# Eight of 32 softmax heads by another road: scores once, exp with queries on partitions, 32x32 transposes on VectorE, product with v in sixteen 32x32 tiles

## The chip, the cores and the metric

The kernel runs on one core of a Trainium2 chip. The time is the device time of one execution in microseconds, from the first to the last instruction; three runs were taken of the kernel before. The engines are TensorE (PE in the profile, its weight loads PEld), VectorE (DVE), ScalarE (ACT), GpSimd (POOL) and SyncE (SP), which issues all DMAs of this kernel in the order in which they are written.

## The reference

```python
# x: 2048 x 1024, 32 heads of 32; all in fp32
def _A_ref(x, wqkv, wo):                    # linear attention
    pq, pk = phi(q), phi(k)                 # phi(t) = where(t > 0, t + 1, exp(t)) + 1e-6
    kv = jnp.einsum("bhsd,bhse->bhde", pk, v)
    z = jnp.einsum("bhsd->bhd", pk)
    o = (pq @ kv) / (pq @ z + 1e-6)
    return o @ wo
def _B_ref(x, wqkv, wo):                    # softmax attention
    scores = jnp.einsum("bhqd,bhkd->bhqk", q, k) * (Dh ** -0.5)
    o = jnp.einsum("bhqk,bhkd->bhqd", _softmax(scores, axis=-1), v)
    return o @ wo
g = sigmoid((x * gate_w).sum(-1, keepdims=True))
return g * _A_ref(x, A_wqkv, A_wo) + (1 - g) * _B_ref(x, B_wqkv, B_wo)
```

## The kernel before

**Linear work.** Each fp32 product with a weight matrix is three matmuls of 128x128 by 128x512 on operands split into a high and a low part (`three`, L151 to L153). A "unit" is one tile of 128 rows times 512 columns: 8 steps over the inner dimension, 24 matmuls. Eighty units lie in the first part (v of heads 0 to 15: 16 units, then q and k of branch B: 64), and 144 come later through the generator `linear`: v of the other heads (16), keys and values of branch A ("kv", 64), queries of A ("q", 32), output of A ("o", 32). The last 32, B's output, come through `output`.
From "kv" on a unit needs the split x of its rows from DRAM (`load_xp`, L473), in one of two buffers. The q stage also rebuilds A's output weights (`mix`, L559, whose parts are stored by L569) and turns its result by four transposes per unit (`queries`, L597). Each kv unit is followed by eight products of 32 x 32 (L498).

**A softmax head, before.** Scores are computed twice. `maxima` has queries on the partitions: 64 matmuls of 128x512 (L791), each with a maximum over its row on VectorE (L796). The negated maxima are turned (L807), and go as two extra rows into the q operand, so that the second pass gives scores less their maximum. `heads_` has keys on the partitions: 64 matmuls (L942), each with an exp on ScalarE (L946) into one of seven tiles `pr`. Three times a head, `av` multiplies five or six of these tiles with v: four matmuls of 32 columns of v by 512 queries side by side in column strips, per block of 128 keys (L1038; each fp32 matmul is two records in the profile). The sum over keys is made by elementwise adds of the `pr` tiles: their first 1536 columns on GpSimd (L987, L991; 1792 columns for heads that begin while `linear` is at "q"), the rest on VectorE (L998, L1000), then a matmul with ones (L844), reciprocals (L851) and a product (L854).

**What sets the order.** Nothing is scheduled by the machine: every engine runs the list that the program wrote. A planner in the kernel writes it, from costs per instruction (`MM`, `AV` and so on) and a clock for each engine (`T`). It advances four generators, "lin", "max", "head", "out", and each time takes the one furthest behind its due time (`behind`, `AHEAD`); VectorE work that may wait is put off and filled in (`defer`, `fill`). Eight PSUM banks: six in a ring for single products, two (4 and 7) held for `av` and VectorE's sums. The head loop starts when the v units of heads 16 to 31 and one head's maxima plus 12 are done, and "lin" is then spread over all 32 heads by rates per score (2.6 matmuls in the q stage).

Of the kernel before, what the change touches and what calls it, by code (L numbers as in the profile page):

```python
# [9 lines left out]
F32 = mybir.dt.float32  # L10
# [21 lines left out]
AHEAD = {"head": 0, "max": 6, "lin": 9, "out": 0}  # L32
# [9 lines left out]
NMID = 14  # L42


@with_exitstack
def kernel(
# [50 lines left out]
    v_d = [dram.tile([P, NT, C], F32, name=f"v{c}") for c in range(NQC)]  # L97
    wa_d = [[[dram.tile([HK, P, C], F32, name=f"wa{p}_{a}_{c}") for c in range(NQC)] for a in range(NK // HK)]
# [18 lines left out]
    dn = [sb.tile([P, C // DH], F32, name=f"dn{i}") for i in range(2)]  # L117

# [96 lines left out]
    RING = [0, 1, 2, 3, 5, 6]  # L215
# [98 lines left out]
    def v_out(c, t, ps):  # L314
        va = mid[10 + t % 2]
        nc.scalar.copy(va, ps)  # L316
        nc.sync.dma_start(v_d[c][:, t, :], va)

# [78 lines left out]
    for n, (g, j, sec) in enumerate(order):  # L397
# [7 lines left out]
        split(hi, lo, ps, nc.vector)  # L405
# [26 lines left out]
    lin_kind = [chunks[0][0]]  # L432

# [29 lines left out]
    def load_xp(n):  # L463
        if n in xp_done:
            return
        xp_done.add(n)
        i, t = units[n]
        kind = chunks[i][0]
        xp_ready[n % 2] = 0.0
        if kind != "v":  # L470
            xp_ready[n % 2] = T["pe"] + 4.0
            for p, src in enumerate(oA_d if kind == "o" else xs):
                nc.sync.dma_start(f32(blocks(xp_t[n % 2], p)), src[t])  # L473
# [102 lines left out]
    def keysum(c):  # L576

        yield lambda: both(bank_at(), z_end[c % 2])
# [32 lines left out]
    def linear():  # L611
# [4 lines left out]
        for n, (i, t) in enumerate(units):  # L616
            kind, c = chunks[i]
            follow = chunks[i + 1] if i + 1 < len(chunks) else None
            xp = xp_t[n % 2]
            yield bank_at  # L620
# [8 lines left out]
            if n == (TPC if kind == "v" else 0):  # L629
                load_head(0)  # L630
                load_v(0)
            if n == (TPC + 1 if kind == "v" else 0):
                load_head(1)
                load_v(1)
            for k in range(NK):
                yield lambda: ended(w_left[k], w_ready[k], xp_ready[n % 2])
                need(w_left[k])
                stat = xstat(t, k) if kind == "v" else [blocks(xp, p)[:, k] for p in range(2)]
# [4 lines left out]
                if k == 0 and kind == "v" and c == NQC - 1 and NT - 4 < t < NT - 1:  # L643
                    load_xp(n + 3)
                if k == 0 and n + 7 == len(units) and not o_main[0]:
                    load_o(0)
# [14 lines left out]
                if follow and t == NT - 1:  # L661
                    split_w(*follow, k, *coming_w.popleft(), nc.vector if kind == "v" else nc.gpsimd)
# [6 lines left out]
            if kind == "v":  # L669
                give(b, use("act", 0.5, T["pe"] + LATENCY["pe"]))  # L670
                v_out(c, t, ps)
            elif kind == "kv":
# [18 lines left out]
                if t == NT - 1:  # L691
                    extra = keysum(c)
            elif kind == "q":
# [584 lines left out]
```

## Time and profile before

| | us |
|---|---|
| median of three runs (2920.92 to 2924.22) | 2921.34 |
| span of the profiled execution | 2921.0 |
| mean granted TensorE clock | 0.995 |
| the 80 units of the first part end at about | 442 |
| second-pass scores (L942) | 547 to 2724 |
| after them, what is left of B's output and its storing | 2724 to 2921 |

A row of the timeline or of a group names line, engine, operation, output<-inputs, shape and count; "mean ns" is the length of one record, and since matmuls are pipelined, the distance from one start to the next is what one costs.

### The profile page before, as it was taken

The page shows a single profiled execution, that of the slowest core. Times are in us where ns is not written, and L with a number is a line of the kernel's source. Part 1 is how long each engine was busy: PE and PEld are TensorE (multiplying, and loading weights), DVE is VectorE, ACT ScalarE, POOL GpSimd, SP SyncE. Part 2 cuts the span into 40 slices and gives each one's busy share as a digit, 9 for nine tenths or more (in the row PEclk, how much of TensorE's full clock was granted, in tenths as well). Part 3 has the DMA queues.
Part 4 walks back from the last instruction along what each step waited for, and adds up shares of the span by engine and source line. Part 5 has one row for each costly group of instructions (what it writes and reads, how often), then busy time and mean ns, then how long its engine had stood idle before and what let it go on. Part 6 is the DMA issues. An engine that isn't in the chain of part 4 may idle for free.

```text
span 2921.0 us, 44021 instructions
## 1 busy us (share of the span) xinstructions
PE 2885.7 (99%) x15936; PEld 2073.3 (71%) x15936; DVE 2055.2 (70%) x3451; ACT 1522.7 (52%) x2840; POOL 1772.2 (61%) x582
## 2 busy tenths in 40 slices
PE   9999999999999999999999999789999999999999
PEld 8888888766666666666666767566676666666787
DVE  3222114788888888888888888678888888887522
ACT  4111111466666667666666666556666666666410
POOL 0000001388898889988898888568778878785000
PEclk9999999999999999999999999999999999999999
DMA  6687333322242234233423234545455443523542
GB/s 195 213 268 233 122 116 101 115 87 90 89 132 89 90 91 120 75 89 96 125 90 91 90 117 145 162 157 160 151 157 183 130 145 121 158 87 130 181 154 80
DMA packets 282142, 381.67 MB, mean 131 GB/s; under 512 B 91786, under 2 KB 168074, under 8 KB 278794
## 3 DMA queue, kind: packets, MB, share of 16 engines
q1 hardware_dynamic: 281924, 378.85, 41.9%
q8 instruction: 126, 2.06, 0.3%
q14 instruction: 92, 0.75, 0.1%
HBM read 268.70 MB, written 108.79 MB: 129 GB/s over the span
## 4 chain that ended last, share of the span: by engine, by line
PE 95%; DMA 2%; DVE 1%; ACT 0%; SPq 0%; issue 0%; ACTq 0%
PE bank L942 16%; PE bank L791 16%; PE bank L151 16%; PE bank L153 15%; PE bank L152 15%; PE bank L1038 15%; PE bank L844 1%; DMA big<-xs 0%; PE bank L597 0%; DMA wa<-mid 0%; PE bank L498 0%; DMA big<-oA 0%; DVE big L1004 0%; DMA mid<-in_a_wqkv 0%; DMA big<-in_a_wo 0%; DVE mx L796 0%
## 5 line engine op out<-in xcount | busy, mean ns | idle before, releaser
L991 POOL TENSOR_TENSOR big<-big,big 128x1536 f32<-128x1536 f32 (+1 forms) x434 | 1557.4, 3588 | 209.5 <-ACT big L946 187.4
L796 DVE TENSOR_REDUCE mx<-bank 128x1 f32<-128x512 f32 x2048 | 1312.1, 682 | 334.0 <-PE bank L791 329.9
L946 ACT ACTIVATE big<-bank 128x512 f32<-128x512 f32 x2048 | 1182.1, 602 | 526.7 <-PE bank L942 459.2
L151 PE MATMUL bank<-big,big 128*128 128x512 f32 x2048 | 802.5, 392 | 25.1 <-DMA big<-xs 21.2
L942 PE MATMUL bank<-big,big 128*128 128x512 f32 x2048 | 810.7, 397 | 1.8 <-ACT big L946 1.7
L791 PE MATMUL bank<-big,big 128*128 128x512 f32 x2048 | 803.7, 393 | 2.8 <-ACT mid L316 2.6
L153 PE MATMUL bank<-big,big 128*128 128x512 f32 x2048 | 800.5, 391 | 0.4 <-DVE big L258 0.4
L152 PE MATMUL bank<-big,big 128*128 128x512 f32 x2048 | 800.5, 391 | 0.0
L942 PEld LDWEIGHTS bank<-big,big 128*128 128x128 f32 x2048 | 384.8, 188 | 159.0 <-issue 62.0
L151 PEld LDWEIGHTS bank<-big,big 128*128 128x128 f32 x2048 | 385.4, 188 | 115.2 <-issue 18.9
L1038 PE MATMUL bank<-big,mid 128*32 128x512 f32 x4096 | 459.2, 593 | 0.0
L791 PEld LDWEIGHTS bank<-big,big 128*128 128x128 f32 x2048 | 385.6, 188 | 86.6 <-ACT big L946 3.7
L153 PEld LDWEIGHTS bank<-big,big 128*128 128x128 f32 x2048 | 385.2, 188 | 82.8 <-DVE big L258 1.3
L152 PEld LDWEIGHTS bank<-big,big 128*128 128x128 f32 x2048 | 385.4, 188 | 80.1
L746 POOL MEMSET big<- 32x2048 f32 x3 | 5.4, 1809 | 530.8 <-PE bank L152 459.6
L1038 PEld LDWEIGHTS bank<-big,mid 128*32 128x32 f32 x4096 | 127.7, 110 | 263.7 <-issue 263.7
L1000 DVE TENSOR_TENSOR bank<-bank,big 128x512 f32<-128x512 f32 (+1 forms) x434 | 280.9, 647 | 7.8 <-ACT big L946 6.2
L258 DVE TENSOR_TENSOR mid<-bank,mid 128x512 fp32r<-128x512 f32 x64 | 44.3, 692 | 263.2 <-ACT mid L257 263.2
L987 POOL TENSOR_TENSOR big<-big,big 128x1536 f32<-128x1536 f32 (+1 forms) x31 | 111.7, 3602 | 136.2 <-ACT big L946 136.2
L257 ACT CAST mid<-bank 128x512 fp32r<-128x512 f32 x64 | 37.7, 590 | 291.4 <-PE bank L153 286.5
L851 DVE RECIPROCAL bank<-bank 128x128 f32<-128x128 f32 x128 | 123.4, 964 | 3.5 <-PE bank L844 0.4
L258 DVE TENSOR_TENSOR big<-mid,big 128x512 fp32r<-128x512 f32 x96 | 64.0, 687 | 75.9 <-ACT big L257 75.8
(72 smaller groups left out, 977.9 us busy)
## 6 DMA issues: line engine op xcount, KB each, us to landing
big<-xs SPq DMA_DIRECT2D x192, 512.0 KB
qk<-mid SPq DMA_DIRECT2D x128, 256.0 KB
big<-oA SPq DMA_DIRECT2D x64, 512.0 KB
big<-qk SPq DMA_DIRECT2D x96, 256.0 KB
big<-qk SPq DMA_DIRECT2D x384, 64.0 KB
xs<-big SPq DMA_DIRECT2D x64, 256.0 KB
oA<-mid SPq DMA_DIRECT2D x64, 256.0 KB
mid<-in_b_wqkv SPq DMA_DIRECT2D x48, 256.0 KB
```

Of the source, the lines that this page charges most:

```text
L151: yield nc.tensor.matmul(ps, sh, mh_, start=(kt == 0), stop=False)
L152: yield nc.tensor.matmul(ps, sh, ml_, start=False, stop=False)
L153: yield nc.tensor.matmul(ps, sl, mh_, start=False, stop=(kt == NK - 1))
L791: nc.tensor.matmul(bank[b], q[:, t * P:(t + 1) * P], k[:, j * C:(j + 1) * C], start=True, stop=True)
L796: nc.vector.tensor_reduce(m[:, t, j:j + 1], bank[b], AX.X, ALU.max)
L851: nc.vector.reciprocal(pl[:, sl], pl[:, sl])
L942: nc.tensor.matmul(bank[b], k[:, t * P:(t + 1) * P], q[:, j * C:(j + 1) * C], start=True, stop=True)
L946: nc.scalar.activation(pr_t[i][:, j * C:(j + 1) * C], bank[b], AF.Exp, scale=SCALE)
L987: nc.gpsimd.tensor_add(lacc[:, :qp], pr(0)[:, :qp], pr(1)[:, :qp])
L991: nc.gpsimd.tensor_add(lacc[:, :qp], lacc[:, :qp], pr(t)[:, :qp])
L1000: nc.vector.tensor_add(lacc[:, qp:] if t == NT - 1 else l_b[:, :n], l_b[:, :n], src)
L1038: nc.tensor.matmul(av_b[j * DH:(j + 1) * DH, :], v[:, t, :], pr(t)[:, j * C:(j + 1) * C], start=(t == 0), stop=(t == NT - 1))
```

## The change

Heads 0 to 7 (`NB = 8`) leave the old road; heads 8 to 31 keep it.

- **Scores once** (`bheads`). For each quarter of the queries (512) and each of its four blocks of 128 there are four matmuls of 128 queries by 512 keys, with the same operands as in `maxima`. VectorE takes the negated maximum of each row of 512 keys, ScalarE computes exp(score - maximum) with that maximum as a bias per partition and sums the row (`accum_out`), and VectorE transposes the result in blocks of 32x32 into a tile laid out by key blocks. The maximum is that of the 512 keys alone. The scale is moved into q (`nc.scalar.mul`).
- **Product with v** (`burst`). Once a quarter is complete (16 scores), 256 matmuls of 32x32 by 32x128 follow in one piece, on all 16 tiles of the array: row strip a takes key or query block a, column strip c the keys' quarter c, four PSUM banks. ScalarE copies the four results.
- **Weights and sum** (`weigh`). After a head's four quarters its parts are weighted with exp(maximum of 512 - overall maximum) / sum: small operations on [128, 64], four transposes, four matmuls of 128x512 that spread the factors, four products on GpSimd, and four matmuls that add the parts.
- **Dropped for these heads:** the second score pass with its exp, the turned maxima, `av`, the adds on GpSimd and VectorE, the matmul with ones, the reciprocals.
- **Order.** A new generator "score" is advanced while less than `FEED = 2.4` us of VectorE work is waiting. All eight banks are in the ring until it ends. "lin" fills the rest of that stage with v and kv units only; q waits. v of heads 16 to 31 now reads x back from DRAM as kv does. Then `maxima` and the old head loop run for 24 heads, with q, o and what is left of kv at one rate.
- **Data.** v of the first 16 heads is stored a second time by rows of 32 (four DMAs per tile of 128 rows).

```diff
-AHEAD = {"head": 0, "max": 6, "lin": 9, "out": 0}
+AHEAD = {"head": 0, "max": 6, "lin": 9, "out": 0, "score": 0}
+NB = 8
+EXPB, TRB, AVB, OEV = 0.68, 0.6, 4.3, 0.3
+FEED = 2.4
-    RING = [0, 1, 2, 3, 5, 6]
+    RING = list(range(8))
...
+        if c == 0:
+            for i in range(TPC):
+                nc.sync.dma_start(vh_d[:, :, t * TPC + i, :].rearrange("h i d -> i h d"),
+                                  va[i * DH:(i + 1) * DH, :].rearrange("p (h d) -> p h d", d=DH))
...
+    def burst():
+        n = bursts.popleft()
+        h, J = divmod(n, NJ)
+        bs = [take() for _ in range(4)]
+        end = use("pe", AVB, *(free[b] for b in bs))
+        v = ft[14].rearrange("p (b d) -> p b d", d=DH)
+        for m in range(C // DH):
+            for c in range(NJ):
+                for a in range(4):
+                    rows = slice(a * DH, (a + 1) * DH)
+                    nc.tensor.matmul(bank[bs[a]][c * DH:(c + 1) * DH, :P], v[rows, c * (C // DH) + m, :],
+                                     place(n, c)[rows, m], start=(m == 0), stop=(m == C // DH - 1))
...
+    def bheads():
...
+            for i in range(TPC):
+                for j in range(NJ):
...
+                    nc.tensor.matmul(bank[b], bq[:, J * C + i * P:J * C + (i + 1) * P], k[:, j * C:(j + 1) * C],
+                                     start=True, stop=True)
...
+                    nc.vector.tensor_reduce(m[:, col], bank[b], AX.X, ALU.max, negate=True)
...
+                    nc.scalar.activation(src, bank[b], AF.Exp, bias=m[:, col], accum_out=lb[h % 2][:, col])
...
+                        nc.vector.transpose(place(n, j)[:, :, i, :], src.rearrange("p (m q) -> p m q", q=DH))
...
-    streams = {"lin": linear(), "max": maxima(), "head": heads_(), "out": output()}
+    streams = {"lin": linear(), "score": bheads(), "max": maxima(), "head": heads_(), "out": output()}
...
-    steps = H * NT * NJ
+    steps = (H - NB) * NT * NJ
...
+        if name == "score":
+            work = sum(it.cost for it in later if it.at < T["pe"] + 1.0)
+            return 50.0 if max(T["dve"] - T["pe"], 0.0) + work < FEED else -100.0
         if not begun[0]:
             if name == "lin":
-                return 0.0 if lin_done[0] < warm + 8 * pace else -100.0
+                return 0.0 if lin_next[0] in ("v", "kv") else -100.0
...
+            rate[0] = (warm + sum(cost.values()) - lin_done[0] - RESERVE) / steps
```

TensorE's list, before, in the kv stage: second-pass scores (L942), maxima (L791), linear work (L151 to L153), the eight small products of a kv unit (L498) and a run of `av` (L1038).

```order
L942 MATMUL bank_243<-big_210,big_211 128x512
L151 MATMUL bank_249<-big_226,big_213 128x512
L791 MATMUL bank_245<-big_209,big_222 128x512
L498 MATMUL bank_248<-mid_232,mid_236 32x32 x8
L1038 MATMUL bank_247<-big_3494,mid_241 32x512 x4
L1038 MATMUL bank_247<-big_3495,mid_241 32x512 x4
...
L942 MATMUL bank_244<-big_210,big_211 128x512
L791 MATMUL bank_243<-big_209,big_222 128x512
```

The same stage now, for one of heads 0 to 7: scores (L979), linear work (L161 to L163), kv products (L515), and the first and last rows of a burst (L865).

```order
L515 MATMUL bank_254<-mid_242,mid_244 32x32 x8
L161 MATMUL bank_258<-big_232,big_221 128x512
L979 MATMUL bank_253<-big_219,big_216 128x512
L162 MATMUL bank_258<-big_232,big_221 128x512
L163 MATMUL bank_258<-big_232,big_221 128x512
...
L163 MATMUL bank_258<-big_234,big_221 128x512
L865 MATMUL bank_255<-big_2915,big_2925 32x128
L865 MATMUL bank_254<-big_2915,big_2925 32x128
...
L865 MATMUL bank_253<-big_2918,big_2925 32x128
L515 MATMUL bank_251<-mid_240,mid_244 32x32 x8
L979 MATMUL bank_257<-big_219,big_216 128x512
```

A quarter now has 16 scores among about 60 linear matmuls and then 256 burst matmuls without a break, where before every pair of scores shared its place with one linear matmul. In the whole stage there are 512 scores, 32 bursts and 1908 linear matmuls up to the start of the old head loop; 1500 linear ones are left for its 24 heads and 816 for the last part, as many as before.

VectorE's list, before, in a head: maxima (L796) and adds (L1000).

```order
L1000 TENSOR_TENSOR bank_250<-bank_250,big_3493 128x512
L796 TENSOR_REDUCE mx_200<-bank_249 128x1
L796 TENSOR_REDUCE mx_200<-bank_244 128x1
L796 TENSOR_REDUCE mx_200<-bank_246 128x1
L1000 TENSOR_TENSOR bank_250<-bank_250,big_3494 128x512
```

Now, in heads 0 to 7: maxima (L985), transposes (L995), and the kv stage's operations (L694).

```order
L985 TENSOR_REDUCE mx_202<-bank_258 128x1
L995 STREAM_TRANSPOSE big_2921<-big_2923 128x16x32
L995 STREAM_TRANSPOSE big_2922<-big_2923 128x16x32
L995 STREAM_TRANSPOSE big_2915<-big_2923 128x16x32
...
L694 SCALAR_TENSOR_TENSOR mid_241<-mid_241,bank_253 128x256
L985 TENSOR_REDUCE mx_202<-bank_252 128x1
```

One maximum in four carried an add beside it; now each maximum carries a transpose of the same 512 elements.

SP's list where the first part ends, now: the last stores of q and k, the loads of x for the first two units, and then 24 loads of q and k for head 0, a row of x2 being two of them.

```order
L424 DMA qk_0_7_151<-mid_244 128x512
L425 DMA qk_1_7_159<-mid_246 128x512
L490 DMA big_220<-xs_0_63 128x1024
L490 DMA big_220<-xs_0_79 128x1024
L490 DMA big_221<-xs_1_64 128x1024
L490 DMA big_221<-xs_1_80 128x1024
L776 DMA big_217<-qk_0_0_144 32x512
L776 DMA big_217<-qk_1_0_152 32x512
L776 DMA big_217<-qk_0_0_144 32x512 x2
```

Before, the same place went on with v units out of SBUF, and the loads for head 0 came while these ran.

GpSimd's list in the old head loop, before, kv stage (L987 opens a head).

```order
L991 TENSOR_TENSOR big_3498<-big_3498,big_3497 128x1536
L686 TENSOR_TENSOR mid_235<-mid_235,mid_232 128x256
L987 TENSOR_TENSOR big_3499<-big_3491,big_3492 128x1536
L991 TENSOR_TENSOR big_3499<-big_3499,big_3493 128x1536
L991 TENSOR_TENSOR big_3499<-big_3499,big_3494 128x1536
```

Now, second of the 24 heads (L1238 opens a head).

```order
L1242 TENSOR_TENSOR big_2922<-big_2922,big_2918 128x1536
L1238 TENSOR_TENSOR big_2923<-big_2919,big_2920 128x1792
L1242 TENSOR_TENSOR big_2923<-big_2923,big_2921 128x1792
L1242 TENSOR_TENSOR big_2923<-big_2923,big_2915 128x1792
L1242 TENSOR_TENSOR big_2923<-big_2923,big_2916 128x1792
```

The longer adds, which belonged to 5 of 32 heads, now belong to 12 of 24, because q is spread over more heads.

More of the change, by code (lines that the diff above doesn't have):

```diff
@@ L468, in load_xp @@
         kind = chunks[i][0]
[L469 to L473, printed above, removed]
+        xp_ready[n % 2] = T["pe"] + 4.0
+        for p, src in enumerate(oA_d if kind == "o" else xs):
+            nc.sync.dma_start(f32(blocks(xp_t[n % 2], p)), src[t])
     def phi(ps, e, n):
@@ L661, in linear @@
                 if follow and t == NT - 1:
[L662 removed]
+                    split_w(*follow, k, *coming_w.popleft(), nc.gpsimd)
                     if k + LEAD_W < NK:
@@ L1200, in head_left @@
         return "head" in streams
+    changed = False
+    prepare()
     advance("lin")
+    for j in range(NJ):
+        load_k(0, j)
+    advance("score")
+    load_bv(0)
+    for j in range(NJ):
+        load_k(1, j)
     advance("max")
```

292 lines of the change are left out of this document (246 added, 46 removed).

## The prediction

> **What bounds the kernel now.** I read the page first: the busy shares, the slices, the chain that ended last, and the instruction queue of TensorE.
>
> ```profile
> PE 2885.7 (99%) x15936; PEld 2073.3 (71%) x15936; DVE 2055.2 (70%) x3451; ACT 1522.7 (52%) x2840; POOL 1772.2 (61%) x582
> DVE  3222114788888888888888888678888888887522
> POOL 0000001388898889988898888568778878785000
> PE 95%; DMA 2%; DVE 1%; ACT 0%; SPq 0%; issue 0%; ACTq 0%
> q8 instruction: 126, 2.06, 0.3%
> ```
>
> TensorE is busy from end to end and makes 95% of the chain. VectorE's 70% hides two kernels: a fifth to a third in the first fifth, eight tenths after it. So I asked for windows inside the three stages of the head loop (kv, q, o).
>
> ```profile
> 600.00:1700.00 1100.00, 1100.00 (x6863) 748.49 (x6862) 943.51 (x1607) 721.96 (x1393) 965.15 (x341) 1.00 0.32 96
> 1830.00:2150.00 320.00, 296.90 (x1614) 208.30 (x1607) 250.80 (x439) 187.36 (x356) 218.25 (x60) 0.96 0.49 156
> 2250.00:2650.00 400.00, 398.84 (x2176) 271.00 (x2175) 335.96 (x543) 250.47 (x435) 324.36 (x94) 1.00 0.41 125
> ```
>
> The columns after the length are PE, PEld, DVE, ACT, POOL. In kv TensorE never rests while VectorE is busy for 86% and GpSimd for 88%. In q TensorE idles 23 of 320 us although no other engine is over 78%; the waits of that stage say why.
>
> ```profile
> PE bank L151 <- DMA big<-xs: 21.2, 2, 15.1
> 1838.36 2.36 SPq L569 DMA_DIRECT2D wa<-mid  x1
> 1851.71 2.73 SPq L473 DMA_DIRECT2D big<-xs  x2
> ```
>
> Linear work waited twice for x, behind stores of `mix` that kept SP 2.4 us each. Everywhere else the kernel is worth what TensorE must do. Unit prices come from starts in TensorE's timeline.
>
> ```profile
> 567.68 0.33 PE L498 MATMUL bank<-mid,mid 128*32 128x32 f32 x16
> 567.83 4.48 PE L1038 MATMUL bank<-big,mid 128*32 128x512 f32 x40
> 572.24 0.50 PE L942 MATMUL bank<-big,big 128*128 128x512 f32 x1
> 572.80 0.40 PE L942 MATMUL bank<-big,big 128*128 128x512 f32 x1
> ...
> 574.88 0.39 PE L151 MATMUL bank<-big,big 128*128 128x512 f32 x1
> 1830.43 0.25 PEld L559 LDWEIGHTS bank<-big,kvb 32*32 32x32 f32 x32 [0.84 <-DVE mid L702]
> 1830.43 1.16 PE L559 MATMUL bank<-big,kvb 32*32 32x512 f32 x32
> 1831.52 1.92 PE L1038 MATMUL bank<-big,mid 128*32 128x512 f32 x16
> 1833.37 0.50 PE L151 MATMUL bank<-big,big 128*128 128x512 f32 x1
> ```
>
> From 572.80 to 574.88 lie nine matmuls of 128x512: 0.231 us each. A run of `av` with 40 records (five key blocks) takes 572.24 - 567.83 = 4.41, one with 16 (two blocks) 1.85: a block costs (4.41 - 1.85) / 3 = 0.853 and a run 0.144 more. `mix` uses just the form that the change relies on, sixteen 32x32 tiles: 16 products by 512 columns in 1831.52 - 1830.43 = 1.09 us, 0.853 + 0.24. So sixteen tiles run in the time of four.
>
> ```profile
> L844 PE MATMUL bank<-big,ones 128*32 128x512 f32 x264 | 35.0, 604 | 0.0
> L597 PE MATMUL bank<-ident,mid 128*128 128x128 f32 x128 | 20.2, 281 | 0.0
> L807 PE MATMUL bank<-ident,mneg 128*16 128x128 f32 x32 | 8.7, 271 | 0.0
> ```
>
> These give 35.0 / 33 = 1.06 us for a head's matmul with ones, 20.2 / 32 = 0.63 for four transposes, 0.27 for the turned maxima.
>
> **What goes from TensorE**, for each of 8 heads: 64 second scores, 64 x 0.231 = 14.8; `av`, 16 x 0.853 + 3 x 0.144 = 14.1; the matmul with ones 1.1; the turned maxima 0.3. Together 30.2.
>
> **What comes.** A burst has 16 rounds on 16 tiles, 128 columns a round: 0.853 / 4 = 0.213 of streaming, 3.41 for all, and 0.24 at its edges as in `mix`: 3.65 at least. It also issues 512 matmul records and 512 loads. The kv products show the narrowest spacing with short matmuls: 16 pairs in 567.83 - 567.68 = 0.15 us, 9.4 ns a pair, which makes 512 x 9.4 = 4.8, 5.05 with the edges; `mix` starts its 32 loads within 0.25 us. Far above stands 16 x 1.09 = 17.4, no overlap between rounds. I take 4.1 + 0.24 = 4.34, between the two near bounds, since streaming and issue demand about the same. Four bursts are 17.4. The weighting adds 0.63 (transposes) + 4 x 0.231 + 1.06 (adding four parts, same shape as L844) = 2.6. Together 20.0.
>
> So a head saves 10.2, eight save **82 us**. At the lowest and highest near bound of a burst (-0.69, +0.71 each, 32 bursts) this becomes 104 or 59.
>
> [...]
>
> **New waits.** *VectorE.* Its back-to-back prices:
>
> ```profile
> 710.62 3.07 DVE L796 TENSOR_REDUCE mx<-bank 128x1 f32<-128x512 f32 x5
> 714.21 0.68 DVE L796 TENSOR_REDUCE mx<-bank 128x1 f32<-128x512 f32 x1
> 2726.60 9.72 DVE L1004 TENSOR_TENSOR big<-big,big 128x512 f32<-128x512 f32 x16
> L681 DVE SCALAR_TENSOR_TENSOR mid<-mid,bank 128x256 f32<-128x256 f32 x64 | 26.6, 415 | 4.7 <-ACT bank L480 4.1
> L507 DVE TENSOR_TENSOR kvb<-bank,kvb 128x64 f32<-128x64 f32 x60 | 12.9, 215 | 0.2
> ```
>
> A maximum costs (3.07 - 0.68) / 4 = 0.598; 512 elements from SBUF to SBUF, (9.72 - 0.68) / 15 = 0.60. No transpose stands in the trace; 0.60 bounds it below, twice that, 1.20, above. I take 0.63: the nearest row, same length and places, and a little for filling a 32x32 block. [...]
> A quarter then needs 16 x (0.598 + 0.63) = 19.6 on VectorE, 1.9 kv units at 0.42 + 0.22 = 1.2, 0.1 for `weigh`: 20.9. TensorE in the same quarter: 16 scores and 1908 / 32 = 60 linear matmuls, 76 x 0.231 = 17.5; kv products 0.4; the burst 4.3; weighting 0.6: 22.8. TensorE stays the longer one, at 92% for VectorE, where kv before had 86%. But a burst needs the last transpose of its quarter, and from the last score to it lie a maximum, an exp and a transpose, some 2 us, with mostly five to eleven other matmuls listed between: up to 0.8 us of wait, I take 0.5, x 32 = **15 us** (5 to 60, the top if each quarter also loses the slack of 1.9).
>
> ```profile
> L946 ACT ACTIVATE big<-bank 128x512 f32<-128x512 f32 x2048 | 1182.1, 602 | 526.7 <-PE bank L942 459.2 <-POOL big L991 3.4 <-issue 2.5
> L377 DVE DVE_READ_ACCUMULATOR big<-big,zrep 128x1 f32 x32 | 2.7, 83 | 0.0
> ```
>
> ScalarE's exp, 0.60, may carry a row sum at some 0.08 (VectorE's price): 16 x 0.68 = 10.9 and copies of 1.2 a quarter leave room for kv. Costed at nothing; VectorE's 20.9 covers it.
>
> *GpSimd.* In heads 0 to 7 it is nearly idle. Later 12 of 24 heads have adds of 1792 columns.
>
> ```profile
> 1837.92 16.51 POOL L991 TENSOR_TENSOR big<-big,big 128x1792 f32<-128x1792 f32 x4 [6.26 <-ACT big L946]
> ```
>
> One costs 16.51 / 4 = 4.13, a head's 15 adds 61.9. TensorE in such a head: 64 + 64 scores and about 61 linear, 189 x 0.231 = 43.7; `av` 14.1; ones 1.1; turning 2.5 x 0.63 + 0.3 = 1.9: 60.8. GpSimd becomes the longer one by 1.1; with 0.9 of jitter, 12 x 2.0 = **24 us** (10 to 50). The other 12 heads have 1536 columns and room.
>
> *SP at the end of the first part.* v of heads 16 to 31 now needs x from DRAM, queued behind the last q and k stores, and the first score's 24 loads come behind that.
>
> ```profile
> L762 SPq DMA_DIRECT2D big<-qk x384: 302/412/1794, 466.3 to 2609.0; - x192
> L473 SPq DMA_DIRECT2D big<-xs x192: 319/354/3505, 527.2 to 2174.8; - x192
> ```
>
> 4 x 0.35 + 24 x 0.41 = 11.3 us of issue and about 4 for landing, against 27 linear matmuls (6.2 us) that can run: **10 us** (5 to 20). Storing v twice, 64 issues during the first v stage, is hidden under SP's free time.
>
> *Given back.* In q one unit now lasts 24 us instead of some 10, since linear work is spread evenly. x comes two units ahead, so `mix`'s stores no longer hold it up: **-18** of the 21.2 (0 to -21).
>
> **The sum.** -82 + 15 + 24 + 10 - 18 = -51; the profiled span 2921.0 becomes 2870.0. The median shown is 0.3 above that span, which is less than I can resolve.
>
> **Rivals.** *No new waits* beyond their lower ends: -82 + 5 + 10 + 5 - 21 = -83, 2838. For: VectorE has 8% of room. Against: three engines over 90% in the same stages.
> *Transposes too slow.* From T = 0.75 a quarter is VectorE's: 16 x (0.598 + 0.75) + 1.3 = 22.9. Each 0.1 beyond costs 32 x 1.6 = 51 us, so the gain is gone at T = 0.85. At 1.20 a quarter takes 30.1, 7.3 more than TensorE's 22.8: 2870 + 32 x 7.3 = 3104, slower. For: no row shows a transpose. Against: every other 512-element row costs 0.60.
> *Instruction supply.* The queue row gives 31872 records (matmuls and loads) / 126 = 253 per packet, and 0.3% of 16 x 2921 us / 126 = 1.1 us per packet. A burst's 1024 records are four packets, 4.4 us, just its own length. If half of them must be waited for with a second packet time each, it grows to about 6.5: 32 x 2.2 = 70, 2940, slower from 5.9 on. [...]
> [...]
> *GpSimd holds the later heads* at 4 us each: 24 more becomes 48 and the give-back fails, 2912, within reach of no change.
>
> **How the numbers follow.** Forecast 0.57 (itself 2850 to 2900), no new waits 0.13, transposes 0.12, supply 0.06, slow issue 0.02, GpSimd 0.10. A difference of 0.2% (6 us) is about what can be told. Faster: 0.55 + 0.13 + half of GpSimd's 0.10, less a little: 0.72; same: 0.05; slower: 0.23, nearly all of transposes, supply and slow issue and the rest of GpSimd's. The range runs from the case without waits, 2838, to 2965, which takes in supply and transposes up to T = 0.94.
>
> **What would show it.** Right: a burst of about 4.3 us from its first start to the next line's; transposes at 0.6 to 0.65; TensorE over 95% busy in heads 0 to 7; heads of 62 us in q with GpSimd full; a gap near 442. Wrong: VectorE full in heads 0 to 7 with TensorE waiting for it before each burst (transposes), gaps inside bursts put down to issue (supply), or bursts near 13 us.

## The result, and the profile after

The kernel before took 2921.49 us (2920.92 to 2924.22), the changed one 3346.78 us (3338.30 to 3352.82), four runs each: a ratio of 1.145 with a 95% interval of 1.1431 to 1.1468. The prediction was 2870, so the time is 477 us longer than forecast, the profiled span 466 (3336.5 against 2870.0). From the page of the changed kernel, the busy shares, three slice rows, the instruction queue and the chain:

```profile
PE 3083.8 (92%) x30840; PEld 2174.2 (65%) x30840; DVE 2205.5 (66%) x3810; ACT 1618.8 (49%) x3528; POOL 1472.2 (44%) x528
PE   9999978888888888878999999999999999999999
DVE  3222147575575665657888788888888888898622
PEclk9999999799989998899999999999999999999999
q8 instruction: 242, 3.96, 0.5%
PE 75%; DVE 13%; issue 6%; ACT 3%; DMA 2%; POOL 0%; SPq 0%; DVEq 0%; ACTq 0%
```

TensorE was to be busy for over 95% in heads 0 to 7; from the 7th slice to the 17th it shows 8. "Issue", time in which it waited for nothing that the profile shows, went from 0% of the chain to 6%, and the instruction queue from 126 packets to 242. VectorE, which the prediction feared, rests more there than before. The windows (heads 0 to 7, then heads in q, then heads in o; columns as in the prediction, the granted clock is the number after POOL's):

```profile
458.40:1500.00 1041.60, 864.85 (x19712) 679.51 (x19713) 654.10 (x1171) 519.78 (x1492) 125.41 (x143) 0.92 0.35 112
1900.00:2450.00 550.00, 527.84 (x2679) 311.39 (x2677) 462.85 (x815) 330.34 (x635) 493.94 (x129) 1.00 0.31 96
2550.00:3050.00 500.00, 496.60 (x2709) 319.96 (x2711) 433.74 (x711) 314.96 (x561) 424.61 (x123) 1.00 0.38 112
```

VectorE is busy 63% in heads 0 to 7, and the clock is granted at 0.92. The groups that the disputed prices rest on (busy time, mean ns, then idle time ahead):

```profile
L995 DVE STREAM_TRANSPOSE big<-big 128x512 f32<-128x512 f32 x512 | 340.1, 687 | 0.4 <-ACT big L992 0.2
L992 ACT ACTIVATE big<-bank,mx 128x512 f32<-128x512 f32 x512 | 349.1, 688 | 131.4 <-DVE big L995 70.0
L865 PE MATMUL bank<-big,big 32*32 32x128 f32 x16384 | 272.0, 304 | 157.4 <-issue 153.9
```

A transpose's record is 0.687 us long; back to back they start 0.61 us apart, which is their price, near the 0.63 taken. The bursts (L865) stand still for 157 us, 154 of it for issue. One of them in the timeline:

```profile
705.84 0.39 PE L163 MATMUL bank<-big,big 128*128 128x512 f32 x1
706.16 2.74 PE L865 MATMUL bank<-big,big 32*32 32x128 f32 x192
712.58 2.59 PE L865 MATMUL bank<-big,big 32*32 32x128 f32 x128 [3.68 <-issue]
716.58 2.82 PE L865 MATMUL bank<-big,big 32*32 32x128 f32 x128 [1.41 <-issue]
720.03 1.52 PE L865 MATMUL bank<-big,big 32*32 32x128 f32 x64 [0.64 <-issue]
721.49 0.44 PE L515 MATMUL bank<-mid,mid 128*32 128x32 f32 x16
```

It takes 721.49 - 706.16 = 15.3 us instead of 4.34. Twice the piece between two gaps is 128 records long: with a load each, 256 instructions, one packet of the instruction queue (61680 records / 242 packets = 255). The trace bears this out for the whole stage: of the 98 places in the bursts where a record starts over 0.3 us after the one before, 92 (181.6 of 185.6 us) end 1.0 to 1.8 us after a packet of that queue has ended, where chance would have some 12% there; two such places in one burst always lie 128 records apart (60 of 60), and the other six wait for VectorE's transposes. All 32 bursts, from a first start to the next line's, sum to 426.0 us, 13.3 each, where the prediction had 32 x 4.34 = 139.

Where the 466 us of the span are, with the prediction's own prices: **287** in the bursts. **62** in the rest of the stretch from 441.7 to 1562.2, when the first old head begins: it lasts 1120.5 - 426.0 = 694.5, and its 2498 matmuls of 128x512 at 0.231, 61 kv products at 0.15, the weighting at 8 x 2.6 and the allowed waits of 15 + 10 make 632. **109** in heads 8 to 31: the sum of (period of a head, less TensorE's own work in it by its counts and the prediction's spacings) is 160 us over 23 periods where it was 45 over 31 before, and 45 + 24 - 18 = 51 was forecast. 8 us are in none of these.

### The profile page after: what moved, and what is told of

Same layout as the page of the kernel before. It is cut to its first block, busy times and chain, and to the rows that moved or that the text cites. A ratio compares the mean times of both kernels' runs of the same rounds, so it can differ in the third digit from the quotient of the medians.

```text
span 3336.5 us, 75056 instructions
## 1 busy us (share of the span) xinstructions
PE 3083.8 (92%) x30840; PEld 2174.2 (65%) x30840; DVE 2205.5 (66%) x3810; ACT 1618.8 (49%) x3528; POOL 1472.2 (44%) x528
## 4 chain that ended last, share of the span: by engine, by line
PE 75%; DVE 13%; issue 6%; ACT 3%; DMA 2%; POOL 0%; SPq 0%; DVEq 0%; ACTq 0%
PE bank L161 13%; PE bank L163 12%; PE bank L162 12%; PE bank L1289 8%; PE bank L1193 8%; PE bank L865 8%; PE bank L1041 7%; DVE mx L1046 7%; PE bank L979 4%; ACT big L1197 2%; DVE bank L1105 1%; DVE bank L1251 1%; DVE mx L985 1%; DVE big L995 1%; DMA big<-xs 1%
## 5 line engine op out<-in xcount | busy, mean ns | idle before, releaser
L1242 POOL TENSOR_TENSOR big<-big,big 128x1792 f32<-128x1792 f32 (+1 forms) x322 | 1216.9, 3779 | 120.4 <-ACT big L1197 99.5
L1197 ACT ACTIVATE big<-bank 128x512 f32<-128x512 f32 x1536 | 853.1, 608 | 373.7 <-PE bank L1193 332.4
L161 PE MATMUL bank<-big,big 128*128 128x512 f32 x2048 | 811.6, 396 | 25.5 <-DMA big<-xs 24.0
L163 PE MATMUL bank<-big,big 128*128 128x512 f32 x2048 | 805.1, 393 | 0.9 <-DVE big L268 0.4
L162 PE MATMUL bank<-big,big 128*128 128x512 f32 x2048 | 805.3, 393 | 0.0
L1041 PE MATMUL bank<-big,big 128*128 128x512 f32 x1536 | 610.3, 418 | 35.1 <-ACT big L1197 10.3
L1193 PE MATMUL bank<-big,big 128*128 128x512 f32 x1536 | 592.4, 406 | 16.8 <-DMA big<-ml 10.2
L161 PEld LDWEIGHTS bank<-big,big 128*128 128x128 f32 x2048 | 388.9, 190 | 116.9 <-issue 26.3
L163 PEld LDWEIGHTS bank<-big,big 128*128 128x128 f32 x2048 | 387.9, 189 | 86.4 <-DMA big<-xs 2.6
L162 PEld LDWEIGHTS bank<-big,big 128*128 128x128 f32 x2048 | 389.3, 190 | 80.1 <-issue 1.7
L985 DVE TENSOR_REDUCE mx<-bank 128x1 f32<-128x512 f32 x512 | 330.0, 668 | 144.9 <-PE bank L979 144.4
L865 PE MATMUL bank<-big,big 32*32 32x128 f32 x16384 | 272.0, 304 | 157.4 <-issue 153.9
L1041 PEld LDWEIGHTS bank<-big,big 128*128 128x128 f32 x1536 | 288.5, 189 | 196.6 <-DVE mx L1046 79.5
L992 ACT ACTIVATE big<-bank,mx 128x512 f32<-128x512 f32 x512 | 349.1, 688 | 131.4 <-DVE big L995 70.0
L1193 PEld LDWEIGHTS bank<-big,big 128*128 128x128 f32 x1536 | 284.2, 189 | 146.1 <-issue 44.1
L865 PEld LDWEIGHTS bank<-big,big 32*32 32x32 f32 x16384 | 216.1, 109 | 213.6 <-issue 186.4
L1289 PE MATMUL bank<-big,mid 128*32 128x512 f32 x3072 | 347.6, 597 | 0.0
L995 DVE STREAM_TRANSPOSE big<-big 128x512 f32<-128x512 f32 x512 | 340.1, 687 | 0.4 <-ACT big L992 0.2
L699 POOL TENSOR_TENSOR mid<-mid,mid 128x256 f32<-128x256 f32 x60 | 44.0, 733 | 453.9 <-DVE mid L694 430.7
L979 PE MATMUL bank<-big,big 128*128 128x512 f32 x512 | 209.5, 434 | 2.9 <-ACT big L871 0.9
```

Of the source, the lines that this page charges most:

```text
L161: yield nc.tensor.matmul(ps, sh, mh_, start=(kt == 0), stop=False)
L162: yield nc.tensor.matmul(ps, sh, ml_, start=False, stop=False)
L163: yield nc.tensor.matmul(ps, sl, mh_, start=False, stop=(kt == NK - 1))
L865: nc.tensor.matmul(bank[bs[a]][c * DH:(c + 1) * DH, :P], v[rows, c * (C // DH) + m, :], place(n, c)[rows, m], start=(m == 0), stop=(m == C ...
L985: nc.vector.tensor_reduce(m[:, col], bank[b], AX.X, ALU.max, negate=True)
L995: nc.vector.transpose(place(n, j)[:, :, i, :], src.rearrange("p (m q) -> p m q", q=DH))
```

## Experiments on the burst

Theories. *Supply*: TensorE's instructions come in blocks of 256 (the 128 records between two stalls, 60 of 60), some one to two are there ahead (a burst's first stall for a packet comes after 130 to 273 records, 260 to 546 instructions), and a longer run of short instructions waits for each further block. *Pace*: a record of a 32x32 product with its load takes some 26 ns (426.0 us / 16384), whatever stands around it. From here on a time without a ratio is one run, one with a ratio the median of four. Four runs of the changed kernel spread over 14 us, so between single runs a smaller difference says nothing; the sums over bursts and the lengths of heads, from the traces, are compared instead.

**Four pieces** of four rounds, each a task of its own (PARTS = 4, GAP = 2.5):

```
-        for m in range(C // DH):
+        step = C // DH // PARTS
+        for m in range(part * step, part * step + step):
...
+        if part + 1 < PARTS:
+            at = T["pe"] + GAP
+            tasks.append((lambda: at, lambda: piece(n, bs, part + 1)))
+            return
```

> The burst's 16 rounds come in four pieces of four rounds (64 products, 256 instructions with their loads), at least 2.5 us of scores and linear matmuls between two pieces; nothing is left out. Supply theory (TensorE runs dry because its instructions come in blocks of 256, one every 3.5 to 5 us while it waits for them, and only about two are there ahead): the stalls inside the bursts go, what is left is the pace of issue, 13 to 18 ns a product record, 32 x 7 to 9 = 220 to 290 us in place of 426, and the time falls to about 3150 to 3210. Pace theory (512 records at some 26 ns each whatever stands around them): the pieces sum to 426 again, or to 32 x 3 x 0.24 = 23 more for the new edges, and the time stays at 3347 to 3370.

3199.7 us, bursts of 274.4. The waits of TensorE between 500 and 1500, changed kernel, and between 500 and 1350, four pieces (us, times, longest); and a piece in the timeline:

```profile
PE bank L865 <- issue: 152.6, 91, 5.0
```

```profile
PE bank L873 <- issue: 27.3, 27, 2.5
```

```profile
667.42 0.39 PE L163 MATMUL bank<-big,big 128*128 128x512 f32 x1
667.74 1.90 PE L873 MATMUL bank<-big,big 32*32 32x128 f32 x128
669.57 0.46 PE L515 MATMUL bank<-mid,mid 128*32 128x32 f32 x32
```

The stalls fall to a sixth with the same instructions in the same order within a burst. So supply is shown, for 150 of the 287 us (185.6 to 35.6 in the table below). But a piece without a stall still takes 669.57 - 667.74 = 1.83 us, 14.3 ns a record, four of them 7.3 us.

**Eight pieces** (two rounds each, 1.4 us apart).

> As before with eight pieces of two rounds (128 instructions each), at least 1.4 us of other matmuls between them. Supply theory: no stall either, and the first 32 records of each piece go at the 6.7 ns that a burst's first 32 show, so 32 x 8 x (32 x 6.7 + 32 x 13.5 ns) = 165 us plus edges of up to 32 x 7 x 0.24 = 54: 3090 to 3150 in all. Pace theory: 426 plus 54 for edges, about 3400.

3293.5, a miss: bursts of 278.1. Fewer stalls (35.6 to 16.4 us) and a quicker start are paid back at twice as many edges (25.7 to 52.9 us from a piece's last start to the next line's, table below), and one burst in the end was stretched by the order from 1378 to 1478, 100 us that are no price of a piece.

**bf16**, one record a product:

```
-        return ft[PT[n % 2][j]].rearrange(...)
+        return ft[PT[n % 2][j]].bitcast(BF16)[:, :S].rearrange(...)
...
-        v = ft[14].rearrange("p (b d) -> p b d", d=DH)
+        v = vb().rearrange("p (b d) -> p b d", d=DH)
```

> Exp writes bf16, the transposes move bf16 and v is rounded to bf16 once a head, so that a product is one record and not two: 256 products with 256 loads a burst, 512 instructions in place of 1024 (the sums keep less precision). Supply theory: two blocks are about what is there ahead, so at most one stall of some 2.5 us is left in a burst: 256 x 13.5 ns = 3.5 alone, 4 to 6 us with it, 130 to 190 us in all. Pace theory, 26 ns a record: 6.7 us a burst, 213 us, with the time spread evenly over the burst and no stall longer than 1 us. Either way 3100 to 3150 in all; the gaps tell them apart, not the sum.

3088.7, bursts of 163.8, with 33 stalls over 0.3 us in 32 bursts, 2.75 each: supply again. The first stall of a burst comes after 115 to 253 records, 230 to 506 instructions. The steady pace is 8.33 ns a record. In fp32 the commonest distance is twice that, 16.67, but other starts come as pairs, 14 and 3 ns apart, so that behind the first 32 records of a piece the mean is 12.5 to 14.5.

**Two rounds of 16.**

```
-        for m in range(C // DH):
+        for m in (0, C // DH - 1):
```

> Only the first and the last of a burst's 16 rounds are left (32 products, 128 instructions), so seven eighths of the product of heads 0 to 7 are left out; everything else stands. It shows what the rest costs without the burst. Both theories: bursts of about 0.7 us, 32 x 0.7 = 22 us in place of 426, and at most 3347 - 404 = 2943. If the other engines held nothing back in heads 0 to 7 and the later heads went as predicted, it would be 2870 - 32 x 3.6 = 2755; what lies between is owed to the rest: VectorE's 20.9 us a quarter, the clock, and some 120 us in heads 8 to 31.

2981.0: with an eighth of the product (bursts of 38.9 us in all) still slower than before, and above both expectations. The window over its heads 0 to 7:

```profile
500.00:1130.00 630.00, 589.34 (x5058) 444.60 (x5057) 613.49 (x1110) 492.29 (x1423) 121.34 (x137) 0.98 0.50 165
```

VectorE is now busy for 97%: a quarter lasts 20.8 us (623.9 from the second burst to the 32nd, over 30), the prediction's 20.9. So even a burst that cost nothing would bring a quarter to 20.8 us and not to TensorE's own 18.5. And from the first maximum of an old head to the last score lie 1641 us, 1637 in the changed kernel: what is lost there has nothing to do with the bursts.

**Half the columns** and **loops swapped**, both on the four pieces, ask what the steady pace is.

```
-  nc.tensor.matmul(bank[bs[a]][c * DH:(c + 1) * DH, :P], ..., place(n, c)[rows, m], ...)
+  nc.tensor.matmul(bank[bs[a]][c * DH:(c + 1) * DH, :P // 2], ..., place(n, c)[rows, m, :TPC // 2], ...)
```

> The kernel with bursts in four pieces (3199.7 us, pieces of 2.14 us, 274 us in all), but each product moves only 64 of its 128 columns: half of the queries of heads 0 to 7 get no product, while the number of matmul records and weight loads stays. It asks what the steady pace inside a piece is, 16.67 ns a record after a first 32 records at 6.67 ns. Streaming theory (the tiles do not run all at once, so that columns take the time): 8.3 ns a record, pieces of about 1.1 us, 274 becomes some 150 us and the time about 3075. Load theory (each record waits for its own weight load or for issue, whatever it moves): still 16.7 ns, 260 to 275 us, and the time stays within 15 us of 3200.

```
-            for c in range(NJ):
-                for a in range(4):
+            for a in range(4):
+                for c in range(NJ):
```

> The kernel with bursts in four pieces (3199.7), only the two inner loops of the burst swapped: four products in a row now read the same 32 rows and write the same bank in four column strips, where before they went round the four row strips and four banks. Nothing is left out. It asks what the steady 16.67 ns a record comes from. If from tiles that share rows: slower, over 20 ns a record, 300 us and more in bursts. If from changing the bank with each product: nearer to 6.7 ns, 150 to 200 us. If from issue or weight loads that go one after another: unchanged, 265 to 285 us and 3200 within 15.

3195.1 and 3201.5; bursts of 245.6 and 277.4. The swap changes next to nothing (274.4 to 277.4), so neither row nor bank order matters here. Half the columns fit neither theory: the stalls grew, from 35.6 to 59.8, but what is not stall fell by 22%, from 238.8 to 185.8, and a piece without a stall from 1.83 to 1.40 us. A straight line through these two lengths (an estimate) puts 3.4 of the 7.3 us of four pieces on the columns, as much as the prediction's streaming of 3.41, and 3.9 on what does not depend on them, as if the two came one after the other. Whether the 3.9 are issue or loads was not separated; bf16 issues the same load and matmul for each record every 8.33 ns, so issue alone would be no more than that of fp32's 14.3, if a record issues alike in both (not shown). All starts of burst records, sorted by their distance to the next:

```
us in all bursts       sum   over 0.3 us (times)  0.025 to 0.3  under 0.025  last to next line
changed kernel       426.0      185.6 (98)            58.4         173.3          8.7
four pieces          274.4       35.6 (30)            48.0         165.1         25.7
eight pieces         278.1       16.4 (14)            60.0         148.8         52.9
bf16                 163.8       90.9 (33)             8.3          59.0          5.6
four, 64 columns     245.6       59.8 (38)            25.2         140.8         19.8
four, swapped        277.4       36.8 (29)            50.3         164.3         26.0
```

So of a burst's 13.3 us 5.8 are stalls and 7.5 the pace and its edges.

## Experiments on heads 8 to 31

In q a head lasts 69.5 us (mean of 13) where TensorE has 59.2 us of work. TensorE shows little idle time, 22 of 550 us, since its records of 0.39 us, 0.23 apart where nothing waits, cover small delays: of 987 scores that follow a matmul of the same shape, 251 start over 0.3 us after it, against 39 of 1161 before. The waits stand at its weight loads. Changed kernel, 1900 to 2450, against before, 1000 to 1600:

```profile
PEld bank L1041 <- DVE mx L1046: 43.6, 103, 1.4
PEld bank L1041 <- ACT big L1197: 25.0, 65, 0.9
PEld bank L1193 <- DVE mx L1046: 11.1, 32, 0.7
PEld bank L1193 <- ACT big L1197: 9.1, 39, 0.5
```

```profile
PEld bank L791 <- ACT big L946: 2.1, 10, 0.3
PEld bank L942 <- ACT big L946: 2.0, 10, 0.3
```

A score's matmul waits until VectorE's maximum or ScalarE's exp has emptied a PSUM bank: 89 us of 550, against 4 of 600. The prediction's cause was GpSimd's 1792 columns; the rival is the banks, emptied late by a VectorE with 462.85 / 550 x 69.5 = 58 us of work in a head.

**GpSimd eased, VectorE eased, both.**

```
-QP_Q = 7 * 256
+QP_Q = QP
```

```
-                items = [defer(lambda _: own(t), ...)]
+                items = []
+                if t in (0, NT - 1):
+                    items = [defer(lambda _: own(t), ...)]
```

> The changed kernel as it is (3347), but GpSimd adds 1536 columns a key block in q as elsewhere, and VectorE the other 512 instead of 256. GpSimd theory (the old heads in q last 69 us because 15 adds of 4.13 us fill it): a head's adds fall from 62 to 53 us, 13 heads go from 69 to about 62, -90: 3255. VectorE theory (58 us of VectorE in a head for which TensorE needs 60, so that its evacuations come late and PSUM banks with them): 15 x 0.27 = 4 us more on VectorE a head, 13 heads of 72 to 74, 40 to 60 us more: 3390 to 3405.

> The changed kernel, but VectorE adds its 256 (or 512) columns only for the first and the last key block of an old head: 14 of 16 of its part of the row sums are left out. GpSimd's part stays. VectorE theory: 14 x 0.33 = 4.6 us less on VectorE a head in q and 14 x 0.6 = 8 in o; the 13 q heads fall from 69 to 64 or 65 and the time by 50 to 80: about 3280. GpSimd theory: the q heads stay at 68 to 70, the time at 3330 to 3347.

> Both: GpSimd adds 1536 columns in every old head, and VectorE's part of the row sums is left out for 14 of 16 key blocks. Both engines are then eased. VectorE theory: as without VectorE's adds alone, within 10 us (about 3280). GpSimd theory: as with 1536 columns alone, about 3255. If both are near their limits, neither alone gives much and this one does: q heads of 61 to 62, 3240.

The first moves adds from GpSimd to VectorE, the second leaves out 14 of VectorE's 16 adds a head, the third does both: 3344.3, 3297.8 and 3299.7. With both eased:

```profile
1900.00:2450.00 550.00, 534.48 (x2758) 320.87 (x2757) 443.52 (x720) 338.47 (x651) 439.99 (x132) 1.00 0.34 104
```

GpSimd falls from 90% to 80% and nothing follows: it was not the cause. VectorE's relief gives 3 us a head and 49 in all, just under the 50 to 80 expected. But the first gave VectorE 4 us more a head, and that cost next to nothing (heads of 69.8), against the VectorE theory. The amount of its work alone is not the cause either.

**Half of each maximum**, same order.

```
-  nc.vector.tensor_reduce(m[:, t, j:j + 1], bank[b], AX.X, ALU.max)
+  nc.vector.tensor_reduce(m[:, t, j:j + 1], bank[b][:, :C // 2], AX.X, ALU.max)
```

> The changed kernel with the same order, but each of the 1536 maxima of the old heads reads only 256 of the 512 columns that its matmul wrote: half of each maximum is left out, and VectorE frees the PSUM bank some 0.27 us earlier. Bank theory (TensorE's starts in the old heads wait for banks that VectorE empties late, 54 of the 88 us of weight-load waits between 1900 and 2450; VectorE has 58 us of work in a head for which TensorE needs 60): those waits go, the 13 heads in q fall from 69.3 to 62 to 64 us, the whole by 80 to 110 us, to about 3245. Order theory (the heads are long because of the order in which matmuls stand, or because of ScalarE and GpSimd behind them): heads in q stay over 67.5 and the time over 3320.

3293.8, heads in q of 66.4: between the two. Its waits in the same window:

```profile
PEld bank L1041 <- ACT big L1197: 35.9, 94, 1.4
PEld bank L1193 <- ACT big L1197: 26.9, 84, 1.2
...
PEld bank L1041 <- DVE mx L1046: 6.7, 14, 0.9
```

The waits for VectorE go from 55 to some 7 us, as the bank theory has it, and more than half of that comes back as waits for ScalarE, 34 to 63.

**Maxima less delayed by other work.**

```
-                fill(end + LATE)
+                fill(end + 0.4)
```

> The changed kernel; only the rule by which other work of VectorE may stand ahead of a maximum of an old head is tighter: it must end within 0.4 us of the matmul instead of 1.0 (nothing is left out). Bank theory, in the form that banks come free late because other work of VectorE stands ahead of the maxima: fewer waits, heads in q of 66 to 68 us instead of 69.3 and a fall by 30 to 60 us, about 3300. If only VectorE's amount of work counts, not its place: 3335 to 3350.

3301.2, heads in q of 67.4: a hit for banks that come free late because of what stands ahead of them.

**The old rule for linear work** in the changed kernel, and the new one in the kernel before:

```
-            rate[0] = (warm + sum(cost.values()) - lin_done[0] - RESERVE) / steps
+            left = max(warm + cost["kv"] - lin_done[0], 0.0)
+            rates["q"] = 2.6
+            rates["kv"] = rates["o"] = rates["v"] = (left + cost["o"] - RESERVE) / (steps - cost["q"] / rates["q"])
```

> The changed kernel with the rule for linear work of the kernel before: 2.6 linear matmuls a score in q (five heads of some 160), the rest evenly, which leaves some 38 to a head in o. Nothing is left out. Spreading theory (the even rule is what makes the heads in q long): five heads of 82 us and eighteen of about 55, some 60 to 100 us less: 3250 to 3290. Fill theory (a head cannot go far below 62 to 65 us whatever linear work it holds, since VectorE and the PSUM banks need that long for its 128 scores): the heads in o with 38 linear matmuls still last 61 to 65 us though TensorE has 53 us of work in them, and the time does not fall: 3340 to 3400.

```
-    rates = {"q": RATE_Q, "v": 0.0}
-    rates["kv"] = rates["o"] = (cost["kv"] + cost["o"] - RESERVE) / (steps - cost["q"] / RATE_Q)
+    rates = {"v": 0.0}
+    rates["kv"] = rates["q"] = rates["o"] = (sum(cost.values()) - RESERVE) / steps
```

> The kernel before, with only the change's rule for linear work: it is spread evenly over all heads, about 98 matmuls a head, instead of 2.6 matmuls a score in q (five heads of some 150) and 83 to 86 a head elsewhere. No head has queries on partitions. Spreading theory (the even rule itself makes heads in q long, since each q unit keeps banks and VectorE for longer than a dense q does): 8 to 9 heads in q with 7 to 10 us over TensorE's work each, 40 to 60 us slower than before, 2965 to 2985. Fill theory (heads get long only when TensorE's work in them falls towards 60 us, because VectorE's 55 to 60 us then have no room): these heads have 69 us of TensorE work, lose 2 to 4 us each, and the time stays within 15 us of 2921.

3407.4, slower still, just above the fill theory's 3400; and 2934.9 (ratio 1.0039, 1.0024 to 1.0054), within the fill theory's 15 us of before, though its heads in q lose 4 to 10 us and not 2 to 4. The first, over heads in o that hold 38 linear matmuls:

```profile
2220.00:2970.00 750.00, 735.45 (x3623) 401.44 (x3620) 637.93 (x1039) 425.62 (x813) 621.51 (x179) 1.00 0.27 77
```

```profile
PEld bank L1041 <- DVE mx L1046: 70.1, 228, 1.0
PEld bank L1041 <- ACT big L1197: 46.2, 165, 0.7
```

```
period of a head, us (mean)      linear matmuls   period   TensorE's own work
before, in o                          86           64.5         64.6
changed, in o                         65           62.3         59.6
changed with the old rule, in o       38           63.4         53.7
```

Half the linear work, the same length. As ordered here, an old head in o lasts 62 to 64 us on average for its 128 scores (69 in q), and no engine need be full for it: VectorE is at 85%. It is a floor of this order, not a fixed one. Over the last six periods, all in o, a head lasts 61.4 us in the changed kernel, 60.0 with the tighter rule and 59.3 with VectorE's adds left out, where TensorE's own work is some 59.5 each time: with less work on VectorE, or in a better place, TensorE is the bound again. In the kernel before, TensorE's 64.6 us lay just above that length; the change took work out from under it. That the banks make the length is shown by the waits and by what moves them, not by a run with more banks.

## Candidates

**Four such heads, two such heads**: bf16, two pieces, 0.4 us, changed costs for the planner, and NB of 4 or 2. The one with four also has `FEED = 1.5` and an `AHEAD` of 6 for "lin", which were not tried alone.

```
-NB = 8
+NB = 4
```

> A candidate: 4 heads instead of 8 with queries on partitions, bf16 for p and v (one record a product; the sums of those heads keep less precision), each burst in two pieces of 256 instructions 2 us apart, and the tighter rule of 0.4 us ahead of the maxima. Old heads: 28, with some 75 linear matmuls each instead of 61. If TensorE stays the bound: bursts of 2 x 1.6 = 3.2 us, a head saves 30.2 - 4 x 3.2 - 2.6 = 14.8, four 59: 2862. If the old heads cannot go far below the 64.5 us that they had before (bank theory: near their limit on VectorE and PSUM banks), then what the four heads save comes back in the other 28: 2905 to 2950, that is, no better than before.

> The same with 2 heads with queries on partitions and 30 old ones of some 80 linear matmuls each. TensorE as bound: 2921 - 2 x 14.8 = 2891. Bank theory: 2905 to 2935. Beside the kernel with four such heads it says whether the old heads' length or the new heads set the time.

2951.2 (ratio 1.0089, 1.0074 to 1.0104) and 2961.2 (1.0132, 1.0114 to 1.0151): 1% slower than before, with intervals above 1, and 1 and 26 us above the bank theory's ranges, by which two heads should have come nearer to before than four. The old heads are only part of it. With four, by the prediction's prices, the stretch from 441.7 to the first old head is 56 us longer than TensorE's work and the bursts (46.9) in it, where nothing was lost in that place before, and the old heads lose some 30 us more than before; with two it is 40 and some 17. Of the 56, 24 are waits for x; the rest was not found. The same (and the `AHEAD` of 6) with three heads and 2.0, and with four and 1.4 linear matmuls a score in q:

> A candidate: as the kernel with 4 heads with queries on partitions (bf16, two pieces, 0.4 us), but with 3 such heads, and in q 2.0 linear matmuls a score instead of the even rule. Spreading theory: the 57 to 68 us that the heads in q and around mix lost with 2 and 4 such heads fall to about 30: 2915 to 2925, level with before. Fill theory: denser heads in q gain, the sparser ones after them lose, 2940 to 2960 as before.

> The same with 4 heads with queries on partitions and 1.4 linear matmuls a score in q. Beside the same kernel with the even rule (2951.2): spreading theory 2920 to 2935, fill theory 2940 to 2960.

2976.8 (1.0173, 1.0145 to 1.0201) and 2978.8 (1.0189, 1.0174 to 1.0205), above both theories. Each has a single stop that the others lack; in the first:

```profile
ACT mid L618 <- DMA oA<-mid: 22.2, 1, 22.2
```

ScalarE waited 22 us to overwrite a tile whose store was under way, with the exps behind it. If the stop costs its whole length (20.8 us in the second), they would lie at 2955 and 2958 without it, as the fill theory has it; no run shows this. No version beat the kernel before.

## Why the prediction was wrong

- **The burst's price** is the step that failed: "I take 4.1 + 0.24 = 4.34, between the two near bounds". It measured 13.3: 5.8 of stalls, and 7.5 of pace and edges. The lower bound counted streaming alone and the upper one the first 16 starts of a run; a burst's first 32 records do mostly start 6.7 ns apart, but after them the mean is 12.1 to 14.5 by burst (distances over 0.1 us left aside), as if streaming and the rest added up where the prediction had them overlap. Even without a stall, four pieces take 7.3, 1.7 times the price. The far bound, 17.4, is nearer to 13.3 only because of the stalls, which it did not contain. The mix row, sixteen products in 32 records, was too short to show either the pace, which begins after the first 32, or the supply, whose first stall comes after 130.
- **Instruction supply** was the right rival, at the wrong size: "if half of them must be waited for with a second packet time each" gave 2.2 us a burst, the runs show 5.8. A packet takes 1.1 us on its queue (mean of 242), but in the burst at 645.7, which starved, four started 3.5 to 5 us apart (3.2, 8.1, 11.7 and 15.5 us after its first record). Its chance of 0.06 was far too low: a run of 1024 instructions against packets of 253 had no precedent in the trace. The first stall for a packet comes after 130 to 273 fp32 records, 260 to 546 instructions, so that some one to two packets were there ahead, and 29 of the 32 bf16 bursts, of 512 instructions, stall just once.
- **Slow issue**, 0.02 in the prediction, and its "bursts near 13 us": no run shows a pace of issue that makes a burst so long. The 13.3 came near it by luck: 83% of the starts in bursts lie 3 to 17 ns apart, and 185.6 of the 426.0 us are stalls.
- **VectorE** was right: transposes 0.61 apart, a quarter of 20.8 against 20.9 once the bursts had only two rounds, and few waits for them in the bursts (3.4 us, six times).
- **GpSimd, 24 us**, was wrong in its cause and its size. What failed is "TensorE in such a head: ... 60.8" as the length of a head: it took TensorE to be the bound at 60.8 because it was at 64. As ordered, such heads take 62 to 69 us whatever TensorE saves, so what it saves there is not kept.
- **SP's gap** cost 15.3 us of waits for x against 10, as the waits between 441 and 500 show, and the only other wait for x lies between 1500 and 1562:

```profile
PE bank L161 <- DMA big<-xs: 15.3, 2, 8.9
```

```profile
PE bank L161 <- DMA big<-xs: 8.7, 1, 8.7
```

- **Given back** was right, then: none is left in q. But the old heads lost more by other waits.
- The 62 us beside the bursts are the kv products behind them (32.4 instead of 9.2 us, 18 of it waits for issue), and scores 0.29 and linear matmuls 0.243 us apart instead of 0.231; the granted clock of 0.92 is a part of these.

What stays open: what a burst's pace is made of (streaming, issue, loads), what else the candidates lose ahead of the old heads, and why heads in q last longer than those in o: of the 10 us by which they exceed TensorE's work, VectorE's adds left out took 3, halved maxima 3 and their better place 2, each alone; the rest was not found.

## What to carry to other kernels

Price a run of short instructions at its whole length, not by its first starts, and count its instructions against the blocks in which they come: 128 pieces of 256 with other work between them stalled 30 times in all, and 1024 in a row lost 5.8 us on average. Before counting what an engine saves, look for how far the stage could shorten at all in the order that it has: here a head in o stayed at 62 to 64 us with 65 or 38 linear matmuls, though no engine was full. A wait may hide in later starts of an engine that the page calls busy; it shows at its weight loads (here 89 us of 550, beside 22 us of idle time).

## What was not expected of the hardware

Exp with a row sum issues a second instruction, 0.199 us and not 0.08:

```profile
L992 ACT ACTIVATION_READ_ACCUMULATOR big<-bank,mx 128x1 f32 x512 | 101.8, 199 | 0.0
```

A transpose of bf16 takes as long as one of fp32 (688 and 687 ns). After the stop of 6.4 us at 441 TensorE ran at half speed for some 5 us: starts lie 0.43 us apart and then 0.23, and the granted clock from 442 to 458 is 0.79. The 0.92 of heads 0 to 7 is made up of full speed and 20 stretches of 3 to 17 us at 0.5, 160 us in all.

```profile
448.17 0.76 PE L161 MATMUL bank<-big,big 128*128 128x512 f32 x1 [6.43 <-DMA big<-xs]
...
452.48 0.63 PE L163 MATMUL bank<-big,big 128*128 128x512 f32 x1
452.90 0.63 PE L161 MATMUL bank<-big,big 128*128 128x512 f32 x1
...
454.20 0.39 PE L162 MATMUL bank<-big,big 128*128 128x512 f32 x1
454.42 0.39 PE L163 MATMUL bank<-big,big 128*128 128x512 f32 x1
```
